# Query weights loaded plainly and turned by TensorE, late rows on GpSimd's queue, half of the key sums on GpSimd: a change to a two-layer linear-attention and GLU kernel

## The chip, the cores and the metric

The kernel runs on one core of a Trainium2 chip. Its engines work side by side, each on an instruction list of its own that it takes strictly in order, and meet through semaphores: TensorE (PE, matrix products), VectorE (DVE), ScalarE (ACT), GpSimd (POOL) and SyncE (SP, which here only issues DMAs). The metric is the time of one execution on the device, in microseconds (us); less is better.

## The reference

One sequence of 2048 rows (16 tiles of 128) by 512 features, in bf16. Two layers, each with an attention part and a GLU part; both layers use the same weights.

```python
def _A_ref(x, wqkv, w_phi, wo):                  # H = 32 heads, Dh = 16
    q, k, v = x @ wqkv, split by heads
    pq = einsum("bhsd,hdf->bhsf", q, w_phi); pk = the same with k
    phi_q = concat([softmax(pq), softmax(-pq)]); phi_k = concat([softmax(pk), softmax(-pk)])
    kv  = einsum("bhsf,bhsd->bhfd", phi_k, v);  z = phi_k summed over s
    num = einsum("bhqf,bhfd->bhqd", phi_q, kv); den = einsum("bhqf,bhf->bhq", phi_q, z) + 1e-6
    return (num / den) @ wo

def _B_ref(x, W_gate, W_up, W_down):             # F = 1376
    gate = x @ W_gate; up = x @ W_up
    return (relu(gate) * up) @ W_down

x = A_x
x = x + _A_ref(layernorm(x), ...);  x = x + _B_ref(layernorm(x), ...)
x = x + _A_ref(layernorm(x), ...);  x = x + _B_ref(layernorm(x), ...)
```

What sets the shape of the kernel: `kv` and `z` are sums over all 2048 rows, so no query can be answered before the keys and values of all 16 tiles are done.

## The kernel before

Everything stays in SBUF: x (16 tiles), all weights, and rings of buffers for what is in between. `build_kernel` records every operation with `op(...)`: its engine, a function that emits it, what it reads and writes, and two costs of the order's model, `ii` (how long it keeps its engine) and `lat` (when its result is there). `Program.forward` places the operations by a list of ranks, `RANKS`, one number per operation, and `prepare` turns the resulting order into waits on semaphores. `MOVED` lists operations that run on their second engine (`alt`). So the order on each engine is fixed by `RANKS`, `MOVED` and the model's costs; the chip then runs those lists in order, whatever the true times are.

At the start DVE builds an identity matrix, and PE runs 40 small matmuls that compute nothing (L553). `w_phi` is spread into block-diagonal form `BD` (L556, two parts on GpSimd and two on DVE). It is folded into the weights, so that one matmul gives the features before the softmax: `Wkp` = key weights times `BD`, `Wqp` = query weights times `BD` (`compose`, L586 for the matmuls, L462 and L463 for the copies from PSUM on ACT and DVE). This product needs the weights transposed. The key weights are loaded plainly into a part of `Wd` that is still free, and turned by PE (L574). The query weights are turned on the way by four DMA transposes from HBM (L521). SP issues the loads in the order of `LOADS`: x tile 0, key weights in two halves, x tile 1, tiles 2 and 3, value weights, tiles 4 to 7, query weights; then, between the transposes of later work, tiles 8 to 11 and 12 to 15 (`late_x`).

Then for each tile t of layer 0:
- `ln`: statistics and their aggregate on DVE (L600, L601), Ln and Exp on ACT (L603, L605), y on DVE (L620) or, for some tiles from 6 on, on GpSimd (L619; its small `nmr`, L616, is on GpSimd for tiles 6 to 15 in any case, and y waits for it even on DVE). y is turned by PE (L629) for tiles 0 to 3 and by a DMA transpose on SP (L634) for the others.
- `kv_tile`: keys K (L652, tile 0 at L656), two exponentials on ACT (L663), Z = sums of the exponentials in groups of 16 on DVE (L664), 1/Z on ACT by Ln and Exp (L668, L669), norm = their product on DVE (L672); values V (L681), copied to `vaug`, mostly by ACT (L462).
- `kv_sums`: the matmuls that sum over the tiles (L716), in bursts; then a mask on DVE (L724, L727) gives `kvs`.

Queries (`q_chunk`, L696, 16 chunks of four matmuls, exponentials at L700) depend only on y, so they can stand anywhere after it; PE uses some of them to fill the stage of keys and values. Then `attn_tile` for each tile (L749 products with `kvs`, small steps `sm` on GpSimd, DVE and ACT, t and o on DVE or GpSimd, L812 the output product, L815 the residual), and slab by slab the GLU (L842 gate and up, L849, L850, L870; L896 and L898 down; L904 the residual). Layer 1 has the same parts.

Of the kernel before, what the change touches and what calls it, by code (L numbers as in the profile page):

```python
# [12 lines left out]
P = 128  # L13
# [33 lines left out]
class Op:  # L47
    __slots__ = ("i", "eng", "fn", "ii", "lat", "tiles", "uses", "deps", "order", "succ", "start", "end",
                 "dma", "nbytes", "name", "alt", "cnt", "waits", "npend", "ready", "prio", "stream")


class Program:
    SYNC, START = 40.0, 750.0
    DMA_ISSUE, DMA_FIXED, DMA_BW = 470.0, 1500.0, 320.0
# [7 lines left out]
    def op(self, eng, fn, reads=(), writes=(), parts=(), ii=100.0, lat=None, name="", claims=(), after=(), dma=None, nbytes=0, alt=None):  # L62
# [6 lines left out]
        o.dma, o.nbytes, o.alt = dma, nbytes, alt  # L69
# [54 lines left out]
    def busy(self, o):  # L124
        return self.TR_ISSUE if o.dma == "tr" else self.DMA_ISSUE if o.dma else o.ii

    def lat(self, o):
        if o.dma == "tr":
            return self.TR_ISSUE + self.TR_FIXED + o.nbytes
        if o.dma:  # L130
            return self.DMA_ISSUE + self.DMA_FIXED + o.nbytes / self.DMA_BW
        return o.lat
# [21 lines left out]
    def forward(self, prio, look=60.0):  # L154
# [14 lines left out]
        bus = 0.0  # L169
# [31 lines left out]
        while left:  # L201
            pick = None
            for e in ENGINES:
# [5 lines left out]
                for o in ready[e]:  # L209
                    st = o.ready if o.ready > f else f  # L210
                    if low is not None and st > low + look:
                        continue
# [38 lines left out]
            elif o.dma:  # L251
                free[e] = st + self.DMA_ISSUE
                bus = max(bus, free[e]) + o.nbytes / self.DMA_BW
                o.end = bus + self.DMA_FIXED
            else:
                free[e] = st + o.ii
                o.end = st + o.lat
            for t in o.tiles:
# [86 lines left out]
    def prepare(self):  # L345
# [6 lines left out]
        ring = 0  # L352
        last_of = {}
        for o in self.sequence:
# [6 lines left out]
            if o.dma:  # L361
                o.stream = ("d", ring % self.n_dma_sems)
                ring += 1
# [45 lines left out]
def build_kernel(nc, A_x, A_wqkv, A_w_phi, A_wo, B_x, B_W_gate, B_W_up, B_W_down, out):  # L409
# [26 lines left out]
    eps = sb("eps", [1], FP32)  # L436
    kvs = sb("kvs", [8, 144])
# [57 lines left out]
    op("dve", lambda e: e.transpose(coli[:], rowi[:]), reads=rows, writes=[c_col], ii=100, lat=215, name="col")  # L495
    c_idq = [res("identq", q) for q in range(4)]
    for q in range(4):
        sl = slice(32 * q, 32 * q + 32)
        op("dve", lambda e, sl=sl: e.tensor_tensor(ident[sl, sl], rowi[sl, :], coli[sl, :], ALU.is_equal), reads=rows + [c_col, c_id], writes=[c_idq[q]], ii=90, lat=170, name="identq")
# [3 lines left out]
    op("dve", lambda e: e.memset(eps[:], 1e-5), writes=[c_eps], ii=35, lat=70, name="eps")  # L503

    xv = A_x.rearrange("b (t p) d -> p (b t) d", p=P)
    outv = out.rearrange("b (t p) d -> p (b t) d", p=P)
    chain = {"sp": [], "act": []}

    def load(eng, fn, writes, nbytes, name, after=()):
        o = op(eng, fn, parts=writes, dma="load", nbytes=nbytes, name=name, after=chain[eng][-1:] + list(after))  # L510
# [15 lines left out]
    wkn = Wd[:, 0:4, :]  # L526
# [4 lines left out]
    for q, what, *k in LOADS:  # L531
# [8 lines left out]
        elif what == "wvp":  # L540
            load(q, lambda e, k=k: e.dma_start(wv[:, k[0]:k[1], :], A_wqkv[k[0] * P:k[1] * P, 1024:1536].rearrange("(c p) f -> p c f", p=P)), [c_wv], 131072 * (k[1] - k[0]), "wv")
        elif what == "wq":
            for ic in range(4):
                load_wT(t_wq, c_wqT, 0, ic)
    late_x = []
    for t in range(8, 16, 4):
        load_x("sp", t, t + 4)
        late_x.append(chain["sp"][-1])

# [5 lines left out]
    for a in range(4):  # L555
        fn = lambda e, a=a: e.tensor_tensor(BD[:].rearrange("p c (a f b) -> p c a f b", f=16, b=2)[:, :, a], w128[:].unsqueeze(3).to_broadcast([P, 4, 16, 2]),  # L556
                                            m8[:, 2 * a:2 * a + 2].unsqueeze(1).unsqueeze(1).to_broadcast([P, 4, 16, 2]), ALU.mult)
        cost = {"pool": (290.0, 340.0), "dve": (190.0, 280.0)}
        here, other = ("pool", "dve") if a % 2 else ("dve", "pool")
        o_bd = op(here, fn, reads=[c_w128, c_m8], writes=[c_BD[a]], ii=cost[here][0], lat=cost[here][1], name="BD", alt=(other, fn) + cost[other])  # L560

    va_all = p_va.slots
    for i in range(16):
        op("pool", lambda e, i=i: e.memset(va_all[i][:, :, 128:130], 1.0), writes=[res("va1", i)], ii=60, name="vones", after=[o_bd])
    for i in range(2):
        op("pool", lambda e, i=i: e.memset(p_hr.slots[i], 0.0), writes=[res("hr0", i)], ii=500, name="hr0", after=[o_bd])
    op("pool", lambda e: e.tensor_copy(kvs[:, :, 136:144], mask2[:].unsqueeze(1).to_broadcast([P, 8, 8])), reads=[c_m2], writes=[res("kvsm")], ii=200, lat=280, after=[o_bd], name="kvsm")
# [510 lines left out]
```

## Time and profile before

The median of 6 runs is 394.4 us (392.17 to 395.38). The profiled execution took 394.61 us, of which its span, from first to last instruction, is 392.8; TensorE's granted clock was full throughout.

| Engine | busy us | share of the span | instructions |
|---|---|---|---|
| PE | 378.2 | 96% | 2413 |
| DVE | 298.3 | 76% | 641 |
| ACT | 195.3 | 50% | 606 |
| POOL | 42.1 | 11% | 117 |

Busy time by stretch of the span, in us:

| Stretch | PE | DVE | ACT | POOL |
|---|---|---|---|---|
| 0 to 10 | 7.88 | 8.16 | 5.68 | 2.84 |
| 10 to 20 | 8.00 | 8.06 | 8.17 | 0.00 |
| 20 to 30 | 9.41 | 9.65 | 9.66 | 1.72 |
| 30 to 40 | 10.00 | 9.88 | 9.34 | 5.39 |
| 40 to 55 | 14.33 | 14.25 | 12.31 | 0.00 |
| 55 to 90 | 32.29 | 31.39 | 21.77 | 6.65 |
| 90 to 210 | 119.37 | 92.14 | 50.82 | 7.76 |
| 210 to 260 | 47.92 | 42.13 | 34.07 | 4.77 |
| 260 to 392.8 | 128.96 | 82.61 | 43.49 | 13.02 |

A PE that shows busy is not a PE at its peak: a matmul's record includes the time in which its last results run out of the array, so the records of neighbours overlap and short gaps between them do not show. DVE's and ACT's records overlap in the same way, by some 0.1 us. Rows of the timeline give start, duration and a group of equal instructions; what stands in brackets is the idle time before the group and what ended it.

### The profile page before, as it was taken

The page shows a single profiled execution, that of the slowest core. Times are in us where ns is not written, and L with a number is a line of the kernel's source. Part 1 is how long each engine was busy: PE and PEld are TensorE (multiplying, and loading weights), DVE is VectorE, ACT ScalarE, POOL GpSimd, SP SyncE. Part 2 cuts the span into 40 slices and gives each one's busy share as a digit, 9 for nine tenths or more (in the row PEclk, how much of TensorE's full clock was granted, in tenths as well). Part 3 has the DMA queues.
Part 4 walks back from the last instruction along what each step waited for, and adds up shares of the span by engine and source line. Part 5 has one row for each costly group of instructions (what it writes and reads, how often), then busy time and mean ns, then how long its engine had stood idle before and what let it go on. Part 6 is the DMA issues. An engine that isn't in the chain of part 4 may idle for free.

```text
span 392.8 us, 6587 instructions
## 1 busy us (share of the span) xinstructions
PE 378.2 (96%) x2413; PEld 213.1 (54%) x2455; DVE 298.3 (76%) x641; ACT 195.3 (50%) x606; POOL 42.1 (11%) x117
## 2 busy tenths in 40 slices
PE   7799999899999999999999999999999999999996
PEld 6434565667655544444444457477865544544443
DVE  8899979899897769647678996889998648623424
ACT  5899969546544235334334574875634333113120
POOL 2016002111211000000000000233102110000000
PEclk9999999999999999999999999999999999999999
DMA  8464591233213321100202000013532221210102
GB/s 218 54 160 82 133 353 41 43 69 67 55 27 75 61 42 27 35 6 13 42 0 42 15 13 2 5 38 68 69 67 55 54 55 40 48 48 0 43 0 67
DMA packets 63008, 22.89 MB, mean 58 GB/s; under 512 B 53920, under 2 KB 62976, under 8 KB 62976
## 3 DMA queue, kind: packets, MB, share of 16 engines
q1 hardware_dynamic: 60144, 20.40, 24.2%
q10 hardware_dynamic: 2832, 2.08, 1.7%
q8 instruction: 19, 0.31, 0.3%
q14 instruction: 13, 0.11, 0.1%
HBM read 7.91 MB, written 2.10 MB: 25 GB/s over the span
## 4 chain that ended last, share of the span: by engine, by line
PE 78%; DVE 10%; DMA 4%; ACT 3%; SPq 2%; issue 1%; POOL 1%
PE pb L842 34%; PE pb L896 17%; PE pb L812 6%; PE pb L681 4%; PE pb L716 4%; PE pb L652 3%; PE pb L749 3%; PE pb L696 3%; PE pb L870 2%; DMA yT<-y 2%; PE pb L898 2%; DVE stats L600 2%; DVE t L786 2%; DMA yT<-in_A_wqkv_dram 2%; DVE z L664 1%; ACT expq L700 1%
## 5 line engine op out<-in xcount | busy, mean ns | idle before, releaser
L850 DVE TENSOR_TENSOR hT<-gate,pb 128x512 bf16<-128x512 bf16 (+1 forms) x100 | 57.2, 574 | 40.7 <-PE pb L842 36.0
L849 ACT ACTIVATE gate<-pb 128x512 bf16<-128x512 f32 (+1 forms) x100 | 50.9, 509 | 70.4 <-PE pb L842 69.9
L842 PE MATMUL pb<-yT,Wu 128*128 128x512 bf16 (+1 forms) x392 | 83.1, 336 | 0.3
L842 PE MATMUL pb<-yT,Wg 128*128 128x512 bf16 (+1 forms) x396 | 81.5, 336 | 0.3
L896 PE MATMUL pb<-Wd,hT 128*128 128x512 bf16 (+2 forms) x322 | 76.0, 372 | 0.3
L842 PEld LDWEIGHTS pb<-yT,Wg 128*128 128x128 bf16 x400 | 38.5, 98 | 29.2 <-DVE x_sb L815 0.3
L842 PEld LDWEIGHTS pb<-yT,Wu 128*128 128x128 bf16 x400 | 38.5, 98 | 28.7
L896 PEld LDWEIGHTS pb<-Wd,hT 128*128 128x128 bf16 x330 | 31.6, 98 | 35.1 <-ACT gate L849 0.3
L664 DVE TENSOR_REDUCE z<-phik 128x64 f32<-128x1024 bf16 x32 | 38.3, 1207 | 7.3 <-ACT phik L663 7.0
L600 DVE BATCH_NORM_STATS2 stats<-x_sb 128x6 f32<-128x512 bf16 x64 | 43.2, 684 | 0.5
L700 ACT ACTIVATE expq<-pb 128x512 bf16<-128x512 f32 x64 | 36.1, 610 | 13.8 <-PE pb L696 13.8
L663 ACT ACTIVATE phik<-pb 128x512 bf16<-128x512 f32 x64 | 35.6, 611 | 11.0 <-PE pb L652 10.9
L786 DVE TENSOR_TENSOR t<-pb,sm 128x384 bf16<-128x384 f32 x64 | 33.9, 548 | 0.8 <-POOL sm L776 0.5
L812 PE MATMUL pb<-wo,oT 128*128 128x512 bf16 x120 | 31.3, 379 | 2.3 <-ACT sm L775 1.3
L681 PE MATMUL pb<-wv,yT 128*128 128x512 bf16 x125 | 31.6, 379 | 1.6 <-DMA yT<-y 0.8
L603 ACT ACTIVATE lnv<-mv,eps 128x1 f32<-128x1 f32 (+1 forms) x58 | 16.9, 298 | 32.6 <-DVE mv L601 32.2
L904 DVE TENSOR_TENSOR x_sb<-x_sb,pb 128x512 bf16<-128x512 bf16 (+2 forms) x33 | 21.9, 663 | 12.7 <-PE pb L898 12.7
L696 PE MATMUL pb<-yT,Wqp 128*128 128x512 bf16 x124 | 31.0, 379 | 0.6 <-DVE t L786 0.3
L652 PE MATMUL pb<-Wkp,yT 128*128 128x512 bf16 x118 | 30.1, 379 | 0.9 <-DMA yT<-y 0.5
L620 DVE TENSOR_SCALAR y<-x_sb,mv,rstd 128x512 bf16<-128x512 bf16 x59 | 24.9, 424 | 4.6 <-ACT rstd L605 3.8
L763 ACT ACTIVATE sm<-pb 128x48 f32<-128x48 f32 (+1 forms) x96 | 15.6, 212 | 18.9 <-PE pb L749 18.9
L749 PE MATMUL pb<-kvs,expq 128*128 128x144 bf16 x256 | 23.9, 226 | 0.7 <-ACT expq L700 0.6
(77 smaller groups left out, 385.2 us busy)
## 6 DMA issues: line engine op xcount, KB each, us to landing
out_dram<-x_sb ACTq DMA_DIRECT2D x15, 128.0 KB, 1.7
x_sb<-in_A_x_dram SPq DMA_DIRECT2D x3, 512.0 KB, 4.1
Wg<-in_B_W_gate_dram SPq DMA_DIRECT2D x2, 640.0 KB, 7.2
Wu<-in_B_W_up_dram SPq DMA_DIRECT2D x2, 640.0 KB, 8.7
Wd<-in_B_W_down_dram SPq DMA_DIRECT2D x1, 1280.0 KB, 12.9
yT<-y SPq DMA_TRANSPOSE x55, 2.5
Wd<-in_A_wqkv_dram SPq DMA_DIRECT2D x2, 256.0 KB, 2.9
wv<-in_A_wqkv_dram SPq DMA_DIRECT2D x1, 512.0 KB, 6.6
```

Of the source, the lines that this page charges most:

```text
L600: op("dve", lambda e, t=t: e.bn_stats(stats[:, t, :], x_sb[:, t, :]), reads=[res("x", t)], writes=[res("st", t)], ii=600, lat=690, name=f" ...
L652: i = e.matmul(kt.ap(), src.ap()[:, ic, c0:c0 + 128], Wkp[:, ic, :], start=(ic == 0), stop=(ic == 3))
L664: op("dve", lambda e: e.tensor_reduce(zt.ap().rearrange("p (a b) -> p a b", b=2), ft.ap().rearrange("p s (a f b) -> p (s a) b f", f=16, b= ...
L681: i = e.matmul(vt.ap(), src.ap()[:, ic, c0:c0 + 128], wv[:, ic, :], start=(ic == 0), stop=(ic == 3))
L696: i = e.matmul(qt.ap(), Wqp[:, ic, c * 128:(c + 1) * 128], src.ap()[:, ic, :], start=(ic == 0), stop=(ic == 3))
L700: op("act", lambda e, g=g: e.activation(es[g][0].ap(), qt.ap(), ACT.Exp, scale=(1.0, -1.0)[g]), reads=[qr], writes=[es[g][1]], ii=477, lat ...
L786: return e.tensor_tensor(tt_.ap()[:, b, 0:384].rearrange("p (c h d) -> p c h d", h=8, d=16), pt.ap()[:, 0:432].rearrange("p (c w) -> p c w ...
L812: i = e.matmul(wt.ap(), oT_.ap()[:, c, :], wo[:, c, :], start=(c == 0), stop=(c == 3))
L842: i = e.matmul(pt.ap()[:, 0:n], W[:, ic, fc * 128:(fc + 1) * 128], src.ap()[:, ic, a * 128:b * 128], start=(ic == 0), stop=(ic == 3))
L849: op("act", lambda e: e.activation(st_.ap()[:, 0:n], gt.ap()[:, 0:n], ACT.Relu), reads=[gr], writes=[sr], ii=110 + n * .72, lat=230 + n * ...
L850: op("dve", lambda e: e.tensor_tensor(ht.ap()[:, a * 128:b * 128], st_.ap()[:, 0:n], ut.ap()[:, 0:n], ALU.mult), reads=[sr, ur], writes=[h ...
L896: i = e.matmul(pt.ap()[:, 0:n1 - n0], hT[l, s, fc].ap()[:, c:c + 128], Wd[:, fc, n0:n1], start=(fc == 0), stop=False)
```

## The change

- **Query weights**: loaded plainly by one DMA into another free part of `Wd` (`wqn`), sixth on SP where the value weights were, and turned by PE with 16 transposes (`turn`, the key weights' code made general). The four DMA transposes go. The value weights move to the end of `LOADS`.
- **Late rows**: x tiles 8 to 11 and 12 to 15 are loaded from GpSimd's queue, after tiles 4 to 7 have landed.
- **Z**: for tiles 3 to 13 of layer 0 (`POOL_Z`) GpSimd adds the two halves of each group of 16 exponentials into an fp32 tile of 512 columns (in a buffer of the ring `t`), and DVE reduces that over 8.
- **y**: `nmr` is on GpSimd from tile 4 on (`POOL_Y`), but only two y's of layer 0 run there, five before.
- **The order's model**: operations of DVE marked `port` are not placed while one of GpSimd's runs, and the other way round; some costs are new. GpSimd's memsets of `vaug` come after y of tile 0, those of `hr` and the copy of the mask after the keys of tile 8. GpSimd's DMAs have four semaphores of their own.
- **RANKS and MOVED** are new throughout, so the order of all engines is. What results, over the whole program, by the two orders: BD 4 on GpSimd (2 before) and 0 on DVE (2); copies of `Wkp` 4 on ACT (2) and 0 on DVE (2); copies of `vaug` 28 on ACT (23) and 4 on DVE (9), of which in layer 0 14 (16) on ACT; y on GpSimd 2 (5); o on GpSimd 16 (10) and on DVE 16 (22); `sm` steps on GpSimd 51 (67) and on DVE 45 (29). Query chunks that stand ahead of the last L716 of layer 0: 5 (6).

```diff
@@ Program @@
-    DMA_ISSUE, DMA_FIXED, DMA_BW = 470.0, 1500.0, 320.0
+    DMA_FIXED, DMA_BW = 1300.0, 285.0
...
                     st = o.ready if o.ready > f else f
+                    if e == "dve" and o.port and pool_end > st:
+                        st = pool_end
+                    elif e == "pool" and port_end > st:
+                        st = port_end
...
             if o.dma:
-                o.stream = ("d", ring % self.n_dma_sems)
-                ring += 1
+                if e == "pool":
+                    o.stream = ("d", self.n_dma_sems - 4 + soft % 4)
+                    soft += 1
+                else:
+                    o.stream = ("d", ring % (self.n_dma_sems - 4))
+                    ring += 1
@@ build_kernel @@
-    wkn = Wd[:, 0:4, :]
+    wkn, wqn, c_wqn = Wd[:, 0:4, :], Wd[:, 4:8, :], res("wqn")
...
+        elif what == "wqn":
+            load(q, lambda e: e.dma_start(wqn, A_wqkv[:, 0:512].rearrange("(c p) f -> p c f", p=P)), [c_wqn], 524288, "wqn", after=k[0] if k else ())
...
-    late_x = []
-    for t in range(8, 16, 4):
-        load_x("sp", t, t + 4)
-        late_x.append(chain["sp"][-1])
+    for t in (8, 12):
+        k = res("x", 7) if ("sp", "wqn") in LOADS else c_wqT[2 if t == 8 else 3]
+        load("pool", lambda e, t=t: e.dma_start(x_sb[:, t:t + 4, :], xv[:, t:t + 4, :]), [res("x", k) for k in range(t, t + 4)], 524288, f"x{t}", after=k.writers)
...
+    def turn(src, rd, dst, wr, name, engs):
+        for ic in range(4):
+            pt, pres = tile(p_ps, name, ic)
+            def mmt(e, ic=ic, pt=pt):
+                for c in range(4):
+                    i = e.transpose(pt.ap().bitcast(BF16)[:, c * 128:(c + 1) * 128], src(ic)[:, c * 128:(c + 1) * 128], ident[:])
+                return i
+            op("pe", mmt, reads=rd(ic) + c_id, writes=[pres], ii=240, lat=400, name=f"{name} mm")
+            op_copy(engs[ic], lambda ic=ic: dst.ap()[:, :, ic * 128:(ic + 1) * 128], lambda pt=pt: pt.ap().bitcast(BF16)[:, 0:512].rearrange("p (c n) -> p c n", c=4), [pres], [wr[ic]], f"{name} cp", True)
+    turn(lambda ic: wkn[:, ic, :], lambda ic: [c_wkn[ic], c_wd], t_wk, c_wkT, "WkT", ["act", "dve", "act", "dve"])
+    if ("sp", "wqn") in LOADS or ("pool", "wqn") in LOADS:
+        turn(lambda ic: wqn[:, ic, :], lambda ic: [c_wqn, c_wd], t_wq, c_wqT, "WqT", ["act", "dve", "act", "dve"])
...
-        op("dve", lambda e: e.tensor_reduce(zt.ap().rearrange("p (a b) -> p a b", b=2), ft.ap().rearrange("p s (a f b) -> p (s a) b f", f=16, b=2), AX.X, ALU.add),
-           reads=fr2, writes=[zr], ii=1105, lat=1185, name=f"Z{l}.{t}")
+        if (l, t) in POOL_Z:
+            ht_, hr_ = tile(p_t, "zh", l, t)
+            zh = lambda: ht_.ap().rearrange("p a b -> p (a b)").bitcast(FP32)
+            v = lambda: ft.ap().rearrange("p s (a f b) -> p (s a) f b", f=16, b=2)
+            op("pool", lambda e: e.tensor_tensor(zh().rearrange("p (a b f) -> p a f b", f=8, b=2), v()[:, :, 0:8, :], v()[:, :, 8:16, :], ALU.add), reads=fr2, writes=[hr_], ii=1110, lat=1154, name=f"Zp{l}.{t}")
+            op("dve", lambda e: e.tensor_reduce(zt.ap(), zh().rearrange("p (q f) -> p q f", f=8), AX.X, ALU.add), reads=[hr_], writes=[zr], ii=590, lat=670, name=f"Zh{l}.{t}")
+            zr = [zr]
+        else:
...
+    for i in range(16):
+        op("pool", lambda e, i=i: e.memset(va_all[i][:, :, 128:130], 1.0), writes=[res("va1", i)], ii=60, name="vones", after=[yop[0, 0]])
     for t in range(NT):
         kv_tile(0, t)
-    for k, o in enumerate(late_x):
-        pr.behind(o, next(d for d in pr.ops if d.name == f"yT0.{4 + 2 * k}"))
+    for i in range(2):
+        op("pool", lambda e, i=i: e.memset(p_hr.slots[i], 0.0), writes=[res("hr0", i)], ii=500, name="hr0", after=[kop[0, 8]])
...
+POOL_Z = {(0, t) for t in range(3, 14)}
-POOL_Y = {(0, t) for t in range(6, 16)}
+POOL_Y = {(0, t) for t in range(4, 16)}
...
-    ("sp", "x", 0, 1), ("act", "wphi"), ("sp", "wk", 0, 2), ("sp", "wk", 2, 4), ("sp", "x", 1, 2), ("sp", "x", 2, 4), ("sp", "wv"), ("sp", "x", 4, 8), ("sp", "wq"),
+    ("sp", "x", 0, 1), ("act", "wphi"), ("sp", "wk", 0, 2), ("sp", "wk", 2, 4), ("sp", "x", 1, 2), ("sp", "x", 2, 4), ("sp", "wqn"), ("sp", "x", 4, 8), ("sp", "wv"),
```

The `port` mark stands on BD, y, norm, o and the `sm` steps `p`, `den` and `coef`. A switch in `ln` that would put Ln and Exp on GpSimd (`POW_LN`) is empty and emits nothing but one small memset.

## The prediction

> **What bounds it now.** I read the busy row first: PE is busy 96% of the span, but a matmul's record carries its pipeline tail, so I priced PE by the distance between starts in the chain of waits:
>
> ```profile
> 51.47 3.72 PE pb L716 x64
> ...
> 105.17 4.32 PE pb L842 x20
> ```
>
> A 512-column matmul takes 4.32/20 = 0.216 us, a 129-column one 3.72/64 = 0.058. By the same division 256 columns take 0.109, 192 take 0.0825, 144 take 0.063, 128 take 0.056. Times the program's counts (1,344 of 512 columns, 320 of 256, 128 of 192, 256 of 129, 256 of 144, 100 small ones after 40 for warming) this is 372.5 us of PE work. PE's first matmul starts at 1.08 and its last ends at 389.65, so PE stands still for 16 us in all. Taking each group's start in the PE timeline from the end of the work before it places them: 6.2 us before 20, 2.0 from 20 to 40, none from 40 to 60, 3.9 from 60 to 90, 3.1 from 210 to 260, under 1 in the rest. These gaps are all that any change here can win, besides 3 us at the end. The first of them, in PE's timeline (start, duration, group, and the wait before it):
>
> ```profile
> 9.84 1.04 PE L681 MATMUL pb<-wv,yT 128*128 128x512 bf16 x4 [0.73 <-DMA wv<-in_A_wqkv_dram]
> 10.72 0.39 PE L629 MATMUL pb<-ident,y 128*128 128x128 bf16 x4
> 11.98 0.40 PE L586 MATMUL pb<-BD,yT 128*128 128x128 bf16 x4 [0.87 <-DMA yT<-in_A_wqkv_dram]
> 12.21 1.03 PE L652 MATMUL pb<-Wkp,yT 128*128 128x512 bf16 x4
> 14.31 0.40 PE L586 MATMUL pb<-BD,yT 128*128 128x128 bf16 x4 [1.07 <-DMA yT<-in_A_wqkv_dram]
> ```
>
> PE takes its instructions in order. L586 composes the query weights out of the transposed rows that four DMA transposes bring, and what is queued behind it (the keys of tiles 1 to 3) waits too. PE is busy without a gap only from 18. The queue that issues those DMAs:
>
> ```profile
> 3.67 0.51 SPq L515 DMA_DIRECT2D x_sb<-in_A_x_dram  x1
> 4.22 7.27 SPq L521 DMA_TRANSPOSE yT<-in_A_wqkv_dram  x4
> 18.39 1.19 SPq L634 DMA_TRANSPOSE yT<-y  x1
> 19.63 0.58 SPq L515 DMA_DIRECT2D x_sb<-in_A_x_dram  x1
> ...
> 25.80 0.58 SPq L515 DMA_DIRECT2D x_sb<-in_A_x_dram  x1
> ```
>
> From 20 to 54 PE, ACT and DVE are all full: in the windows DVE is busy 9.65 us of 20 to 30, 9.88 of 30 to 40 and 14.25 of 40 to 55. DVE's last norm (L672) ends at 53.69 and PE's last L716 at 55.2, so DVE ends the stage of keys and values, while PE fills its time with query chunks (six before 55.2). A stage that ends earlier thus gains only if PE also loses its gaps.
>
> **The change, part by part.** What moves is read from the two orders, instruction by instruction. Line numbers are those of before.
>
> 1. **Query weights.** Four DMA transposes (7.27 us of SP's queue) go. In wv's old place, sixth on SP, stands a plain load of the same 512 KB, so I take its landing at 9.8, where the row above shows wv's. PE gains 16 transposes: 16 x 0.056 = 0.9 us of work. PE's order is now: key matmuls of tile 0, 12 weight transposes (waiting for that load until 9.8, as L681 did), y1, 4 more, 4 of L586, y2, 4 of L586, y3, keys 1 to 3, values 0 and 1, 4 of L586, values 2 and 3, 4 of L586. The two waits of 0.87 and 1.07 us go. What is late next is ACT, which copies weights and y (0.48 us from one start to the next): five copies from 10.2 end at 12.7; keys 1 to 3 run 11.8 to 14.4, values 0 to 3 and the rest of L586 to 18.3. Before, the same work (keys and values 0 to 3, all L586) was done at 20.07. **Lead: 1.8 us**, the 0.9 us included.
> Of transposes the Trainium skill says (VectorE: DVE Perf Modes, The three transpose paths) that 128x128 takes 390 ns on TensorE and 1309 ns on the DMA crossbar. By it, 16 on PE would cost 6.2 us and turn the lead into a loss; the trace's rows of four take 0.39 us in all when PE has them queued, so I use the row. The crossbar figure is near the 1.2 us of issue here, but one instruction here turns four such blocks.
>
> 2. **Value weights** are now last on SP, behind rows 4 to 7. The window 5 to 10 moved 259 GB/s, which is 2 us for each 512 KB: rows 4 to 7 land at about 11.5 (their stats ran at 11.40 before, from the same place in the queue) and wv at 13.5. PE wants it at 14.4, behind keys 1 to 3: hidden, with 0.9 us to spare.
>
> 3. **Late rows on GpSimd's queue**, both after rows 4 to 7 have landed. Before, they were issued at 19.63 and 25.80 behind SP's transposes, and no wait of DVE stands behind them, so the load itself gains nothing. The trace has no DMA from GpSimd. From below, like SP's (median 4.1 us from issue to landing): 15.5 and 17.5. DVE now wants row 8 at 16.2 and row 12 at 19.5: hidden. The skill speaks against it (SBUF — State Buffer, SBUF: two separate sides): a DMA from GpSimd has its descriptors written by GpSimd's cores and starves while VectorE runs an operation in a 2-port mode. By it each y (0.40 us) in the way holds a load up; at most three of them run between 11.5 and 15, so 1.2 us is the upper end and the load lands by 16.7. Row 8 would then cost DVE 0.5 us at most; I take 0. Behind the two issues stand GpSimd's nmr for tiles 4 to 7, for which y4 on DVE now waits: two issues at SP's 0.58 us end at 12.7, at twice that at 13.8, and y4's other inputs are there at 14.3. Hidden; if an issue took three times SP's, y4 would be 0.7 us late and so would its transpose. SP's own queue is empty from 4.2, so y4's transpose starts when y4 is done (14.8) and lands at 17.3 (2.5 us, the page); PE wants it at 18.3.
>
> 4. **Z on GpSimd.** For tiles 3 to 13 half of L664 becomes a GpSimd add of 512 results, then a half-length DVE reduce. The nearest rows:
>
> ```profile
> L664 DVE TENSOR_REDUCE z<-phik 128x64 f32<-128x1024 bf16 x32 | 38.3, 1207 | 7.3 <-ACT phik L663 7.0
> ...
> L796 POOL TENSOR_TENSOR o<-t 128x512 bf16<-128x512 bf16 x10 | 11.6, 1164 | 25.6 <-DVE t L791 13.7 <-DVE t L786 11.9
> ```
>
> GpSimd: 11 x 1.16 = 12.8 us, with nmr, y and memsets 18.8. DVE in the chain's distances: Z 1.13, half 0.6, norm 0.6, stats 0.615, y 0.33, aggr 0.11. After y4 and y5 (15.1) DVE has 5 Z 5.65, 11 halves 6.6, 16 norms 9.7, 8 stats 4.9, 8 aggr 0.9, 8 y 2.6, three casts 1.8: 32.2 us, so 47.3 without stalls, against 53.69.
> But norm, y and GpSimd shut each other out:
>
> ```profile
> 33.85 1.52 POOL L619 TENSOR_SCALAR y<-x_sb,rstd,nmr 128x512 bf16<-128x512 bf16 x2
> ...
> 34.80 1.70 DVE L672 TENSOR_TENSOR phik<-phik,rz 128x1024 bf16<-128x1024 bf16 x2
> ...
> 39.81 2.48 DVE L672 TENSOR_TENSOR phik<-phik,rz 128x1024 bf16<-128x1024 bf16 x4
> ```
>
> Two norms take 1.28 us alone (four take 2.48); here 1.70, as the first is held until GpSimd ends at 35.37. The skill has it as a lock for the whole instruction (SBUF — State Buffer, Who interferes with whom): by the rule, 24 norms and y's that arrive at random meet GpSimd busy 18.8 of 32.2 us, with half an add (0.58) left: 0.34 each, 8.1 us. By the rows it is less: from 21 to 38 GpSimd worked 5.9 us and DVE lost 0.42 there, 0.45 at 30.11 (a y of 0.85) and 0.34 waiting for nmr, a fifth. A fifth of 18.8 is **3.8 us, my value**, as the new order sets reduces and stats beside the adds; ends 0 and 8.1. The last norm then ends at 51.1 and the last L716 about 1.5 later, 52.6. PE's own sum from 18.3 is 24 key and value groups 20.75, five query chunks 4.3, L716 7.4: 50.8. ACT's (31 exponentials, 14 vaug, 3 Wqp, 10 expq at 0.48, plus small ones 6.7) ends at 47 plus waits. I take 52.8 for the last L716, against 55.2; one query chunk fewer (0.86) is done by then. **Gain 1.6 us**, the lead of part 1 inside it.
>
> 5. **After that.** Now L749 of tiles 0 and 1 follows the last L716 directly; before, one chunk stood between and hid the masking of kvs (54.42 to 56.03). PE waits some 0.8 us there. But two more chunks (11, not 9) are left to fill the 3.9 us of gaps from 60 to 90. I take 1.3 us of those filled: **net gain 0.5**, ends -1 and +1.5. The rest is reordered, with six more o's on GpSimd (1.16 against 0.43) and 16 small sm steps back on DVE: 0, with 1.5 either way, since only 3.5 us of gaps lie there.
>
> 6. **BD** all on GpSimd: 3.32 + 4 x 0.45 = 5.1, DVE 0.6 us less; L586 wants them at 6.4: 0. All four Wkp copies on ACT (2.0 us from 6.7) let the first keys run to 8.9, against 9.1: 0. The moved memsets, 60 semaphores instead of 64 for SP and ACT, and the constants of the order's model run nothing on the path: 0.
>
> **Sum:** 1.6 + 0.5 = 2.1 us from the profiled execution of 394.6 (span 392.8 and 1.8 around it): 392.5. That run lies 0.2 above the median of 394.4, so **392.3**.
>
> **Rivals.**
> - **The port ends the stage** (slower). Place: DVE's norms from 30 to 52. At 8.1 us of stalls the last norm ends at 55.4, L716 at 56.9: 2.5 us past the 54.4 that breaks even (55.2 less the chunk); with part 5 at 0 it gives 396.9. It decides from 5.6 us of stalls, 0.23 per norm and y. For it: GpSimd's share; against: one fifth measured, and ACT paces the tiles at 1.9 us, so stalls can hide. 0.17.
> - **The start was hidden anyway.** The lead is lost again because ACT and DVE set the pace to 54 as before: 394.3. For it: three full engines. 0.14.
> - **No stall to speak of**: the last L716 at 51.3, 1.5 us more, and later gaps shrink by 0.5 more: 390.3. For it: 6.4 us of DVE work gone. 0.19.
> - Mine, 392.3, itself 390.8 to 393.8: 0.50.
>
> **From these:** a measurement of this kernel tells about 0.5% (2 us) from no change, so faster is below 392.4: all 0.19 of the last rival, 0.31 of mine, 0.02 of the hidden start, 0.52. Slower is above 396.4: 0.11 of the port case, and 0.06 of mine and 0.03 of the hidden start where the reordering behind 60 us loses more than part 5 allows: 0.20. Between: 0.28. The range runs from 389.2 to 396.5, from the last rival less the 1.1 left of part 5's bound to just under the port case.
>
> **What will show it.** PE has values 0 to 3 and the whole composition done near 18.3, and no composing matmul waits for a DMA; the first value matmul waits for none either; the last matmul of the kv sums ends near 52.8; norms run longer than 0.69 us where the Z add is on GpSimd, by 3.8 us in sum with the y's; PE stands some 0.8 us between the kv sums and the third group of L749. I am wrong if norms and y's wait over 5.6 us, if the query load lands past 11, or if gaps appear beyond 90 us, where I priced nothing.

## The result and the profile after

| | before | changed |
|---|---|---|
| median, us | 394.42 (391.4 to 395.76, 42 runs) | 391.77 (390.56 to 393.58, 21 runs) |
| ratio, 95% interval | | 0.9939 [0.9925, 0.9953] |
| profiled execution, us (span) | 394.61 (392.8) | 391.08 (389.3) |
| value and key stage: PE's last matmul of the kv sums ends | 55.2 | 51.44 |

The change makes the kernel 0.6% faster, 2.6 us by the medians and 3.5 by the two profiled executions. The forecast was 392.3. Lines of code moved with the change: L585 and L599 turn and compose weights (before L574, L586), L671 and L709 are keys and values (L652, L681), L687 and L688 the two halves of the new Z, L700 the norm (L672), L744 the kv sums (L716), L777 the products (L749), L840 the output product (L812), L898 the rest of gate and up (L870). In some experiments an added line moves them by a few more.

PE's timeline of the changed kernel, at its start and at the end of the stage of keys and values (start, duration, group; in brackets the idle time before it and what ended that):

```profile
9.83 0.84 PE L585 MATMUL pb<-ident,Wd 128*128 128x128 bf16 x12 [0.92 <-DMA Wd<-in_A_wqkv_dram]
...
11.40 0.39 PE L599 MATMUL pb<-BD,yT 128*128 128x128 bf16 x4
...
11.85 2.76 PE L671 MATMUL pb<-Wkp,yT 128*128 128x512 bf16 x11
14.45 1.89 PE L709 MATMUL pb<-wv,yT 128*128 128x512 bf16 x8
...
18.13 0.39 PE L599 MATMUL pb<-BD,yT 128*128 128x128 bf16 x4
...
47.56 3.88 PE L744 MATMUL pb<-vaug,phik 128*128 128x129 bf16 x64
51.27 1.19 PE L777 MATMUL pb<-kvs,expq 128*128 128x144 bf16 x16
52.51 1.67 PE L724 MATMUL pb<-yT,Wqp 128*128 128x512 bf16 x7
```

One wait is left at the start, for the plain load of the query weights. The composition, and with it the keys and values of tiles 0 to 3, is done at 18.4 (18.13 and four times 0.056); before, the same work was done at 20.07. The values at 14.45 wait for no load. From 18.5 to the end of the kv sums PE has no wait over 0.05 us: its own work now ends the stage. DVE's last norm ends at 49.31, 2.1 us ahead of it.

The groups of the changed kernel from 15 to 52 us (busy time, mean ns of one, and the idle time before them with what ended it), DVE's three and then GpSimd's one:

```profile
L700 DVE TENSOR_TENSOR phik<-phik,rz 128x1024 bf16<-128x1024 bf16 x16 | 11.8, 776 | 0.2 <-ACT rz L697 0.2
L688 DVE TENSOR_REDUCE z<-t 128x64 f32<-128x512 f32 x11 | 7.4, 670 | 0.0
...
L639 DVE TENSOR_SCALAR y<-x_sb,mv,rstd 128x512 bf16<-128x512 bf16 x9 | 4.2, 486 | 0.0
```

```profile
L687 POOL TENSOR_TENSOR t<-phik 128x512 f32<-128x512 bf16 x11 | 14.5, 1334 | 4.9 <-DVE z L688 3.8 <-ACT phik L682 1.1
```

DVE still hardly waits in this stage, but has less to do. Norms and y's are longer than alone (681 and 403 ns in an experiment below), and so are GpSimd's adds (1,334 ns; an add that nothing held takes 1,150): DVE and GpSimd hold each other up. Further on stands what I had not priced. The chain of waits around 257 and 309 us (two stretches of one view; start, duration, what):

```profile
257.57 4.11 DMA oT<-o
...
262.03 0.82 PE pb L840 x3
```

```profile
309.35 3.85 DMA yT<-y
313.20 0.05 issue
313.25 0.83 PE pb L898 x8
```

Two DMA transposes take 4.11 and 3.85 us from issue to landing, where the median is 2.5, and PE stands 1.27 and 0.72 us for them. Neither wait is in the profile of before.

### The profile page after: what moved, and what is told of

It reads as the page before. It is cut to its first block, busy times and chain, and to the rows that moved or that the text cites. A ratio compares the mean times of both kernels' runs of the same rounds, so it can differ in the third digit from the quotient of the medians.

```text
span 389.3 us, 6649 instructions
## 1 busy us (share of the span) xinstructions
PE 377.5 (97%) x2427; PEld 214.1 (55%) x2471; DVE 289.8 (74%) x645; ACT 198.6 (51%) x617; POOL 59.1 (15%) x122
## 4 chain that ended last, share of the span: by engine, by line
PE 84%; ACT 5%; DVE 5%; DMA 4%; issue 1%; SPq 1%; POOL 0%
PE pb L870 33%; PE pb L924 17%; PE pb L709 7%; PE pb L671 7%; PE pb L840 6%; PE pb L724 4%; PE pb L744 4%; PE pb L777 3%; ACT expq L728 3%; PE pb L898 2%; PE pb L926 2%; DMA Wd<-in_A_wqkv_dram 2%; DMA oT<-o 1%; DMA yT<-y 1%; DVE x_sb L843 1%
## 5 line engine op out<-in xcount | busy, mean ns | idle before, releaser
L870 PE MATMUL pb<-yT,Wu 128*128 128x512 bf16 (+1 forms) x395 | 82.1, 336 | 0.2
L870 PE MATMUL pb<-yT,Wg 128*128 128x512 bf16 (+1 forms) x397 | 81.0, 336 | 0.3
L924 PE MATMUL pb<-Wd,hT 128*128 128x512 bf16 (+2 forms) x319 | 75.2, 372 | 0.5
L870 PEld LDWEIGHTS pb<-yT,Wg 128*128 128x128 bf16 x400 | 38.6, 98 | 30.3 <-ACT gate L877 0.4
L870 PEld LDWEIGHTS pb<-yT,Wu 128*128 128x128 bf16 x400 | 38.7, 98 | 29.9 <-DVE t L814 0.2
L840 PE MATMUL pb<-wo,oT 128*128 128x512 bf16 x118 | 30.7, 379 | 2.6 <-DMA oT<-o 1.3
L709 PE MATMUL pb<-wv,yT 128*128 128x512 bf16 x126 | 30.8, 379 | 0.1
L724 PE MATMUL pb<-yT,Wqp 128*128 128x512 bf16 x121 | 29.9, 379 | 0.6 <-DVE t L819 0.2
L671 PE MATMUL pb<-Wkp,yT 128*128 128x512 bf16 x119 | 29.6, 379 | 0.3
L804 POOL TENSOR_TENSOR sm<-sm 128x64 f32<-128x64 f32 x18 | 5.8, 324 | 148.1 <-ACT sm L803 148.1
L791 ACT ACTIVATE sm<-pb 128x48 f32<-128x48 f32 (+1 forms) x96 | 16.4, 221 | 21.6 <-PE pb L777 21.3
L691 DVE TENSOR_REDUCE z<-phik 128x64 f32<-128x1024 bf16 x21 | 24.8, 1203 | 0.6 <-ACT phik L682 0.6
```

What stands on the lines that cost most here:

```text
L671: i = e.matmul(kt.ap(), src.ap()[:, ic, c0:c0 + 128], Wkp[:, ic, :], start=(ic == 0), stop=(ic == 3))
L709: i = e.matmul(vt.ap(), src.ap()[:, ic, c0:c0 + 128], wv[:, ic, :], start=(ic == 0), stop=(ic == 3))
L724: i = e.matmul(qt.ap(), Wqp[:, ic, c * 128:(c + 1) * 128], src.ap()[:, ic, :], start=(ic == 0), stop=(ic == 3))
L840: i = e.matmul(wt.ap(), oT_.ap()[:, c, :], wo[:, c, :], start=(c == 0), stop=(c == 3))
L870: i = e.matmul(pt.ap()[:, 0:n], W[:, ic, fc * 128:(fc + 1) * 128], src.ap()[:, ic, a * 128:b * 128], start=(ic == 0), stop=(ic == 3))
L924: i = e.matmul(pt.ap()[:, 0:n1 - n0], hT[l, s, fc].ap()[:, c:c + 128], Wd[:, fc, n0:n1], start=(fc == 0), stop=False)
```

## The experiments

All ran beside the kernel before, whose median was 394.1 to 394.3 in each set. Except where a line says otherwise, an edit keeps the changed kernel's order on every engine.

**Query weights by DMA transposes again.** The sixth load is wv again, the four DMA transposes come back behind it, the 16 transposes on PE and their four copies go.

```diff
-    ..., ("sp", "wqn"), ("sp", "x", 4, 8), ("sp", "wv"),
+    ..., ("sp", "wv"), ("sp", "x", 4, 8), ("sp", "wq"),
```

> The changed kernel with the query weights as before: value weights sixth on SP, then rows 4 to 7, then four DMA transposes of the query weights; PE's 16 transposes and their 4 copies are left out, every other operation keeps its place on its engine. Theory (the query part gives the lead at the start and PE sets the end of the kv stage): the composing matmuls wait for DMA transposes near 12 and 14.3 us, keys 1 to 3 start near 14.5 instead of 11.85, PE has values 0 to 3 done near 20 instead of 18.35, the kv sums end near 53.1 instead of 51.4, time 393.5. Rival (the start is hidden, DVE or ACT set the end of the stage): kv sums still near 51.5, time 391.8.

Measured: 391.26 us (389.25 to 394.01), ratio 0.9923 [0.9887, 0.996]. PE's timeline of this kernel:

```profile
11.74 0.40 PE L599 MATMUL pb<-BD,yT 128*128 128x128 bf16 x4 [1.59 <-DMA yT<-in_A_wqkv_dram]
...
48.78 3.87 PE L744 MATMUL pb<-vaug,phik 128*128 128x129 bf16 x64
```

One wait of 1.59 us at the start is back, not two, and the kv sums end at 52.65, 1.2 later than in the changed kernel, nearly as expected. Yet the whole is no slower: in its profile the two waits after 257 us are missing. The interval is too wide for a figure, but the expected loss did not come. Something after the stage gives the 1.2 us back, and this kernel has 32 instructions fewer on PE.

**Z wholly on DVE.**

```diff
-POOL_Z = {(0, t) for t in range(3, 14)}
+POOL_Z = set()
```

> The changed kernel with Z of tiles 3 to 13 reduced in full on DVE, in the place of the half-length reduce; GpSimd's 11 adds are left out, all else keeps its place. Theory (without GpSimd's help DVE ends the kv stage): DVE has 11 x 0.53 = 5.8 us more of reduces and loses its 2.3 us of port stalls, so its last norm ends near 52.8 instead of 49.3 and the kv sums near 54.7 instead of 51.4; time 394.5 to 395. Rival (PE alone sets the stage and DVE has slack): kv sums within 0.5 us of 51.4, time 391.8 to 392.3.

Measured: 395.81 us, ratio 1.0036 [1.0018, 1.0055]; PE's timeline:

```profile
50.64 5.44 PE L744 MATMUL pb<-vaug,phik 128*128 128x129 bf16 x64 [2.24 <-DVE phik L700]
```

Now PE waits for DVE's norms ahead of the last kv sums, which end at 56.08, 4.6 later; 3.3 had been expected. Moving half of Z is worth about 4 us (395.81 against 391.77), and without it the change gains nothing. Here GpSimd adds nothing, so this trace also has norms and y's alone: means of 681 and 403 ns.

**Late rows in their old places**: from SP's queue, behind the first and the fourth y transpose.

```diff
-        load("pool", lambda e, t=t: e.dma_start(x_sb[:, t:t + 4, :], ...), ..., after=k.writers)
+        load("sp", lambda e, t=t: e.dma_start(x_sb[:, t:t + 4, :], ...), ...)
```

> The changed kernel with rows 8 to 11 and 12 to 15 loaded from SP again, behind the first and the fourth DMA transpose of y as before; all else keeps its place. By the prediction's sentence that the load itself gains nothing: time 391.8, no change. By the rival that the new order lives on early rows: the load of rows 8 to 11 is issued near 16.1 and lands near 20, DVE waits for it some 4 us at 16.2, and unless the stage has slack the kv sums end 2 to 4 us later, time 394 to 395.5.

Measured: 400.78 us, ratio 1.0164 [1.0131, 1.0197]. DVE's timeline:

```profile
19.59 0.69 DVE L613 BATCH_NORM_STATS2 stats<-x_sb 128x6 f32<-128x512 bf16 x1 [3.93 <-DMA x_sb<-in_A_x_dram]
...
27.45 1.28 DVE L613 BATCH_NORM_STATS2 stats<-x_sb 128x6 f32<-128x512 bf16 x2 [5.05 <-DMA x_sb<-in_A_x_dram]
```

The two loads are issued at 15.6 and 23.2 and take 4 us. DVE stands 9 us, and the kv sums end at 60.8. The expectation had counted the first of the two waits alone. The new order wants row 8 at 16.2: it can't do without early rows.

**The same rows early, but from SP's queue**, right behind wv, waiting for rows 4 to 7 as in the changed kernel.

```diff
-        load("pool", lambda e, t=t: ..., after=k.writers)
+        load("sp", lambda e, t=t: ..., after=k.writers)
```

> The changed kernel, with rows 8 to 15 loaded as early as there, but from SP's queue, right behind the value weights, instead of GpSimd's. It tells the queue from the time: e3 changed both. My theory (only the time counts): rows 8 and 12 land by 16.2 and 19.5 from either queue, nothing on SP stands behind these two issues until y4's transpose is wanted at 14.9, and the nmr of tiles 4 to 7 on GpSimd is free of two issues of 0.84 us: 391.8, within 0.8. Rival (GpSimd's queue itself is needed): the two waiting issues hold SP so that y4's transpose is issued past 15.5, or the rows come past 16.5: the kv sums end past 52.5 and it takes 393 or more.

Measured: 391.28 us, ratio 0.9929 [0.9906, 0.9951]. SP's queue and, below, DVE:

```profile
4.76 4.05 SPq L565 DMA_DIRECT2D x_sb<-in_A_x_dram  x2
15.11 1.29 SPq L653 DMA_TRANSPOSE yT<-y  x1
```

```profile
16.45 0.68 DVE L613 BATCH_NORM_STATS2 stats<-x_sb 128x6 f32<-128x512 bf16 x1
```

Row 8 is there when DVE wants it, y4's transpose goes out at 15.1. The time of the load counts (9 us), the queue does not.

**Z on GpSimd in the kernel before**, in that kernel's order, for the same tiles.

```diff
@@ before.py, kv_tile @@
-        op("dve", lambda e: e.tensor_reduce(...), reads=fr2, writes=[zr], ..., name=f"Z{l}.{t}")
+        op("pool", lambda e: e.tensor_tensor(...), reads=fr2, writes=[hr_], ..., name=f"Zp{l}.{t}")
+        op("dve", lambda e: e.tensor_reduce(...), reads=[hr_], writes=[zr], ..., name=f"Zh{l}.{t}")
```

> The kernel before with the Z part alone: Z of tiles 3 to 13 split between GpSimd and DVE, every other operation keeps its place of before. Theory (Z on GpSimd is of use only with a PE order that has no waits of its own): the waits at the start stay, of PE's 2.0 us of gaps from 20 to 40 only some go, time 393.3 to 394.4. Rival (Z on GpSimd is the whole gain): 391.8. Rival (port): DVE's norms and y's wait for GpSimd more than 5 us, time above 395.

Measured: 397.34 us, ratio 1.0076 [1.0048, 1.0103]; the kv sums end at 58.0. Its groups from 20 to 58 us on DVE:

```profile
L679 DVE TENSOR_TENSOR phik<-phik,rz 128x1024 bf16<-128x1024 bf16 x15 | 10.3, 717 | 0.0
L669 DVE TENSOR_REDUCE z<-t 128x64 f32<-128x512 f32 x11 | 7.5, 678 | 7.1 <-POOL t L668 7.1
...
L620 DVE TENSOR_SCALAR y<-x_sb,mv,rstd 128x512 bf16<-128x512 bf16 x5 | 2.4, 495 | 1.5 <-POOL nmr L616 1.5
```

The time is that of the port rival, but the norms are hardly held (717 ns), so the port is not to blame. The old order asks for the short reduce where it asked for the whole one, before GpSimd has the sum: DVE stands 7.1 us for it, and 1.5 for nmr behind it on GpSimd. In this order moving Z costs 3 us; in the new one it is worth 4.

**The fetch of PE's instructions.** The missing waits of the first experiment led to a second theory. In the page of the changed kernel, the DMA queues have these two (packets, MB, share of 16 engines):

```profile
q8 instruction: 19, 0.31, 0.3%
q14 instruction: 13, 0.11, 0.1%
```

The Trainium skill (Runtime: NRT & Kernel Launch, Instruction fetch mechanics) says that an engine's instructions come by DMA in blocks of 16 KB, 256 instructions each, and that this is mostly hidden. The trace fits that for q8 and PE: 19 packets of 16,384 bytes for PE's 4,898 instructions (19 times 256 is 4,864), and from one packet to the next PE starts some 250. No wait of PE in the profile is put down to them. But the DMA engines have other work then. In the records of the single packets, block and transpose lie so (us):

```
kernel            block, took      the transpose's 544 packets                      PE waits
changed           259.65, 0.94     542 in 258.74-259.65, the last two after that    1.27 at 262.03
before            217.34, 0.93     542 in 216.48-217.39, the last two at 218.26     0.76 at 219.42
fewer (below)      34.57, 1.25     542 in  33.74-34.64,  the last two at  35.80     1.54 at  36.99
more (below)      273.70, 1.36     the last 42 at 275.05-275.89, begun 273.51       1.34 at 276.65
```

A transpose has 544 packets, 512 of 256 bytes and 32 of 4. In the first three rows only two packets of 4 bytes come behind the block, in the last row 42 packets, and each time the whole transpose lands late. Which of the 16 DMA engines moved a packet the records do not tell. The rest of the changed kernel's trace fits: of its 87 transposes issued after 20 us, 13 were under way when a block came, and six of these took 3.85 to 4.62 us to land; of the other 74 none took over 3.28.

If this is right, a block comes when PE has had a certain number of instructions. So it can be moved, with the same work, by the warming matmuls at the start: 16 of 256 columns for 32 of 128 (fewer; the zeros that they read are made 256 wide), or 32 of 64 for 16 of 128 (more).

```diff
@@ fewer @@
-    for k in range(WARM):
-        op("pe", lambda e: e.matmul(pt_w.ap()[:, 0:128], wm.ap()[:, 0:128], wm.ap()[:, 0:128], ...), ...)
+    for k in range(24):
+        n = 256 if k < 16 else 128
+        op("pe", lambda e, n=n: e.matmul(pt_w.ap()[:, 0:n], wm.ap()[:, 0:128], wm.ap()[:, 0:n], ...), ...)
@@ more @@
+    for k in range(56):
+        n = 64 if k < 32 else 128
...
```

The changed kernel once more, for comparison:

> The changed kernel itself, run beside the next three for a direct comparison on one chip. All theories: 391.8, within 0.7. In its profiled run PE stood 1.2 us at 260.8 (for an oT transpose that took 4.1 us from issue to landing instead of 2.5) and 0.8 at 312.4 (for a yT transpose). Theory F (fetch): both come from the 16 KB blocks of PE's own instructions that the DMA engines fetch (at 259.65, 0.94 us; at 310.75, 1.02 us), which hold up the last packets of a transpose under way; then this profile shows the fetches at the same places in the program and at least one of the two waits again. Theory C (chance): the waits are scatter, and lie elsewhere or nowhere in this profile.

With fewer and with more instructions:

> The changed kernel, with the first 32 warming matmuls of 128 columns made 16 of 256: the same time at the start, but 32 fewer instructions on PE (16 weight loads and 16 matmuls), so every later block of PE's instructions is fetched some 16 matmuls later in the program (about 1.5 us near 260). Theory F: the fetch near 260 then falls at about 261.2 and the one near 311 at about 312.3, past the transposes that PE waits for; the waits of 1.2 and 0.8 us go and it takes 389.8 to 390.5. Theory C: nothing changes, 391.8.

> The changed kernel, with 16 of the warming matmuls made 32 of 64 columns: the same time at the start, 32 more instructions on PE, so that every fetch comes some 16 matmuls earlier (about 1.5 us near 260: at 258.1, beside the first half of the oT transpose; near 311: at 309.2, between two transposes). Theory F: the wait near 260 shrinks below 0.7 us or goes, the one near 312 goes: 390 to 391.2, if no new collision appears elsewhere. Theory C: 391.8.

| | median, us | lowest to highest | ratio, 95% |
|---|---|---|---|
| changed again | 391.37 | 390.84 to 392.76 | 0.9936 [0.9913, 0.996] |
| 32 fewer | 390.38 | 389.84 to 390.62 | 0.9907 [0.9886, 0.9928] |
| 32 more | 392.99 | 392.02 to 393.6 | 0.9976 [0.996, 0.9992] |

PE's timelines of the three, in this order:

```profile
262.18 1.02 PE L840 MATMUL pb<-wo,oT 128*128 128x512 bf16 x4 [1.17 <-DMA oT<-o]
```

```profile
36.99 1.04 PE L672 MATMUL pb<-Wkp,yT 128*128 128x512 bf16 x4 [1.54 <-DMA yT<-y]
...
261.68 1.03 PE L841 MATMUL pb<-wo,oT 128*128 128x512 bf16 x4
```

```profile
263.42 1.03 PE L841 MATMUL pb<-wo,oT 128*128 128x512 bf16 x4
...
276.65 1.02 PE L841 MATMUL pb<-wo,oT 128*128 128x512 bf16 x4 [1.34 <-DMA oT<-o]
```

Repeated, the changed kernel has the block at 259.88 and the wait at the same matmul; the wait near 313 is down to some 0.3 us. With fewer instructions the block comes at 262.22 and both waits are gone; a new one, at 36.99, is hidden only in part (the kv sums end at 52.5, 0.8 later), and the kernel is 1.0 us faster than the changed one beside it, with no run in common. With more, the block comes at 260.76 and the wait for this product is gone as expected, but blocks meet other transposes: three new waits, 0.69 at 78.81, 0.92 at 111.15 and the one shown, each beside a block. My 390 to 391.2 held only if no new collision came, and three came. Some 0.5 us of its loss comes earlier, though: its kv sums end at 52.2, not 51.7, behind a wait of 0.76 for a norm, and no block is shown to be the cause of that. By L898's start, which is at 259.25, 260.08 and 261.82 in the three kernels, the block moved by +1.5 and by -1.7 us of PE's work, where 1.5 had been expected.

Two readings over all the profiles leave little to chance. Every one with the changed kernel's number of PE instructions (its own two and six of experiments) has this wait, of 0.98 to 1.27 us; the three with another number do not. And from the end of the kv sums to its end the changed kernel takes 337.8 us (337.6 again), the one with fewer 335.7, and the first experiment, also 32 instructions short, 335.7 too.

**The first experiment with the blocks put back**: DMA transposes for the query weights, and the 32 lost instructions made up by warming matmuls of half the width.

> e1 (the changed kernel with the query weights turned by DMA transposes again), with the 32 PE instructions that it lost beside the changed kernel put back as warming matmuls of half the width (16 of 128 columns made 32 of 64). PE's fetches then fall at the same places of the program as in the changed kernel. Theory F: e1 was as fast as the changed kernel only because its fetches missed the transposes; now the start costs its 1.2 us and the later waits return in part or whole: 392.6 to 393.3. Rival: the query part is worth nothing, whatever the fetches: as e1, 391.3.

Measured: 396.18 us (393.14 to 397.59), ratio 1.0058 [1.0033, 1.0082]. Its timeline on PE, and windows of 2 us (busy PE, PEld, DVE, ACT, POOL, then the granted clock, the DMA share and GB/s):

```profile
13.59 0.61 PE L600 MATMUL pb<-BD,yT 128*128 128x128 bf16 x4 [3.72 <-DMA yT<-in_A_wqkv_dram]
...
266.84 1.02 PE L841 MATMUL pb<-wo,oT 128*128 128x512 bf16 x4 [0.98 <-DMA oT<-o]
...
318.34 0.83 PE L899 MATMUL pb<-Wr,yT 128*128 128x192 bf16 x8 [0.79 <-DMA yT<-y]
```

```profile
12.00:14.00 2.00, 0.41 (x5) 0.42 (x6) 1.87 (x7) 0.00 (x0) 0.94 (x2) 0.50 0.86 199
14.00:16.00 2.00, 2.00 (x16) 1.57 (x15) 0.00 (x0) 1.09 (x2) 0.00 (x0) 0.50 1.03 328
```

The two late waits return, as expected, and from the end of the kv sums to its end this kernel takes 337.9 us again. More than expected happens at the start: the block at 10.82 (1.17 us) meets the query weights' own transposes, PE stands 3.72 us instead of 1.59, its granted clock falls to half until about 18, and the kv sums end at 56.5. So the query part is worth 1.2 us at the kv sums where no block meets the transposes and 4.8 (56.5 against 51.7 in the changed kernel again) where one does.

**The kernel before with fewer instructions**, by the same edit.

> The kernel before, with the first 32 warming matmuls of 128 columns made 16 of 256 (32 fewer instructions on PE, the same time at the start), as e6 did to the changed kernel. In the profile of before, the fetch at 12.16 lies on the fourth DMA transpose of the query weights, whose last 43 packets come at 13.24 to 14.09 (PE waits 1.07 us for it), and the fetch at 217.34 on a y transpose whose last two packets come at 218.26 (PE waits 0.76). Theory F: with the fetches some 16 matmuls later both waits go; the second is worth its 0.8 us, the first at most its 1.1, since DVE ends that stage: 392.8 to 393.8, if no new collision appears. Theory C: 394.2.

Measured: 392.91 us (391.92 to 396.04), ratio 0.9982 [0.9961, 1.0004]. PE's timeline:

```profile
11.32 0.40 PE L587 MATMUL pb<-BD,yT 128*128 128x128 bf16 x4 [0.80 <-DMA yT<-in_A_wqkv_dram]
...
12.42 0.39 PE L587 MATMUL pb<-BD,yT 128*128 128x128 bf16 x4
...
72.03 1.02 PE L813 MATMUL pb<-wo,oT 128*128 128x512 bf16 x4 [1.10 <-DMA oT<-o]
```

The kernel before had two such waits of 0.87 and 1.07 us at the start, as the prediction's rows show, and further on this one:

```profile
219.42 1.04 PE L681 MATMUL pb<-wv,yT 128*128 128x512 bf16 x4 [0.76 <-DMA yT<-y]
```

The second at the start and this one are gone, with both blocks elsewhere; a block at 69.71 brings a wait of 1.10 at 72.03. The kv sums end at 53.4, 1.8 earlier, where at most 1.1 had been expected; the composing matmuls also start 0.66 us sooner. The median falls into the expected range; the interval still touches 1, so a gain of the whole is not shown.

**Who holds whom.** Behind each of the eleven Z adds GpSimd does extra work on idle buffers that nothing reads: an add that reads SBUF, or two memsets, which only write. (Two memsets ahead of all this fill the buffers that the add reads.)

```diff
@@ kv_tile, behind Zp: reading @@
+            op("pool", lambda e: e.tensor_tensor(scr[2][0].ap(), scr[0][0].ap(), scr[1][0].ap(), ALU.add), ...)
@@ kv_tile, behind Zp: writing @@
+            [op("pool", lambda e, i=i: e.memset(scr[i][0].ap(), 0.0), ...) for i in range(2)]
```

> The changed kernel, with one more GpSimd add of two bf16 tiles of 512 columns behind each of the eleven Z adds (idle buffers, the result is used nowhere): some 1.16 us each, 12.8 us more GpSimd work that reads SBUF between 16 and 47. Theory P (while GpSimd reads SBUF, DVE's norms and y's are held, and it while they run): the stalls go from 2.3 us to 5 or more, norms average over 0.85 us against 0.776, the kv sums end past 53.5 instead of 51.44: 393.5 to 396. Theory Q (a busy GpSimd alone holds the rest up, since nmr and the next Z add stand behind the extra work): the same loss here and in the next kernel.

> As the one before, but the extra work behind each Z add is two memsets of 512 columns (some 0.52 us each, 11.4 us in all), which write SBUF and read nothing. Theory P: norms stay near 0.78 us, the kv sums end within 1 us of 51.44, below the kernel with the reading add by 1.5 us or more: 391.8 to 392.8. Theory Q: as the one before, within 0.8 us.

Measured: 399.49 us with adds, ratio 1.0133 [1.0108, 1.0157], and 395.06 with memsets, 1.0014 [0.9993, 1.0034]. The kv sums end at 60.6 and 54.4. With adds, a norm on DVE and GpSimd beside it:

```profile
34.49 1.63 DVE L704 TENSOR_TENSOR phik<-phik,rz 128x1024 bf16<-128x1024 bf16 x1
```

```profile
34.38 1.20 POOL L690 TENSOR_TENSOR t<-phik 128x512 f32<-128x512 bf16 x1
35.53 1.60 POOL L691 TENSOR_TENSOR hT<-hT 128x512 bf16<-128x512 bf16 x1
```

The norm begins at 34.49 in the middle of an add, and ends at 36.12, 0.54 us after the add's end at 35.58; the next add, begun at 35.53, takes 1.60 instead of 1.15, since it is held while the norm runs. They take turns, whole instructions long. With memsets:

```profile
32.77 1.62 DVE L702 TENSOR_TENSOR phik<-phik,rz 128x1024 bf16<-128x1024 bf16 x1
...
44.44 0.68 DVE L702 TENSOR_TENSOR phik<-phik,rz 128x1024 bf16<-128x1024 bf16 x1
```

```profile
32.67 1.18 POOL L688 TENSOR_TENSOR t<-phik 128x512 f32<-128x512 bf16 x1
33.79 0.98 POOL L689 MEMSET hT<- 128x512 bf16 x2
...
43.98 0.98 POOL L689 MEMSET hT<- 128x512 bf16 x2
```

A norm beside memsets takes 0.68, as alone; one that meets a Z add is held until 33.85 and then runs beside the memset. That is what the Trainium skill says (SBUF — State Buffer, Who interferes with whom): a DVE instruction with two SBUF inputs contends with a GpSimd instruction that reads SBUF, not with one that only writes it. Neither theory had the sizes right. The memsets cost some 3.3 us against the changed kernel's 391.8 all the same, and the adds 4.4 us more. Without holds eleven adds are 11 x 1.15 = 12.7 us of GpSimd's time, 22 memsets 22 x 0.52 = 11.5: the 1.2 us between them are too little for 4.4, so that is mainly the reads. In the memset kernel the norms from 13 to 50 us average 1,011 ns, though no memset holds one: the Z adds lie otherwise, and five of these 13 norms, which meet one, take 1.36 to 1.64 us (in the changed kernel three norms in all were held, to 0.92, 1.04 and 1.63). That the adds of the changed kernel fall more luckily because they wait 3.8 us for DVE's short reduce is likely from this, but not shown.

## Why the prediction was right, and where not

The time was right (392.3 for 391.8), inside the range and on the right side. Its parts were not all so, and that the number came so near is in part luck.

1. **Query weights: right in the trace, half told in its worth.** The load landed at 9.83 for 9.8, composition and values were done at 18.4 for 18.3. What the lead is worth I had inside the stage's 1.6 us. It is 1.2 at the kv sums. But I took before's waits of 0.87 and 1.07 for the DMA transposes' own slowness; the second is a fetched block (gone in the kernel before with fewer instructions). The part's other worth, 3.6 us more where a block hits those transposes, was in no term.
2. **Value weights: right**, no wait.
3. **Late rows: the landing right, the worth wrong.** They took 4.1 and 5.4 us to land, and row 8's statistics ran at 16.20 without a wait. But "the load itself gains nothing" was read from the order of before, which never waited for them; in the new order it is worth 9 us. Both numbers stood in my own step (row 8 wanted at 16.2, issued at 19.63 before) and I did not subtract them.
4. **Z: right in the mechanism, mis-sized in the stall, and so wrong in what ends the stage.** I put 3.8 us; norms cost (776 - 681) x 16 = 1.5 and y's (486 - 403) x 9 = 0.7, 2.3 in all. The last norm ended at 49.31 for 51.1, the kv sums at 51.44 for 52.8. With 3.8 us of stalls DVE's norms would have ended the stage; with 2.3 PE's own work did, for which my sum had said 50.8. The time is that of the rival without stalls (51.3), but not its reason: there were stalls, and PE hid them. The share of a fifth was read from a stretch with y's on GpSimd, and misread: from 21 to 38 the trace has 7.1 us of GpSimd work, not 5.9, which makes a sixth, or 3.2 us. The rest lies in how the adds fell: 2.3 of 20.3 us of GpSimd work from 15 to 50, a ninth. The loss is also two-sided, which I had not counted: GpSimd's eleven adds lost 0.18 us each, off the path here.
5. **After that: the sum near, the places wrong.** The stage gained 3.8 us, 2.9 with the one chunk fewer; the spans differ by 3.5, so what came later gained 0.6 for my 0.5. But PE stood only 0.2 us at the products, not 0.8 (the 16 of L777 from 51.27 fill 1.0, the next group starts at 52.51). And beyond 90 us, where I said gaps would prove me wrong, there are two of 1.27 and 0.72. These 2.0 us are waits for transposes that a fetched block met. Without them, and without the one such wait of before that went (0.76 at 219.42), the part behind the stage would have gained some 1.8 us (0.6 + 2.0 - 0.76).
6. **BD, copies, memsets: right at 0**, as far as the trace shows: nothing waits for them.

So the forecast was helped by two misses of opposite sign: the stall term 1.5 us too large, and 2 us of waits for transposes with no term at all. Where these two waits are gone (fewer instructions), the changed kernel takes 390.4, outside the 390.8 to 393.8 of my own case. That version beats both kernels, the one before by 0.9% [0.7, 1.1] and the changed one by 1.0 us.

## What to carry to other kernels

In this kernel, with 4,898 instructions on PE, an edit that changed their number by 32 moved the later instruction blocks, and with them which DMA transposes landed 1 to 2 us late. Where a kernel has as long a list and as many transposes, the same is to be looked for: before crediting or blaming an edit for one or two microseconds, look whether a wait elsewhere came or went, and run it with the count of instructions put back. A new order makes new needs: price each load by when the new order wants it, not by whether the old one waited. Work moved to GpSimd cost both engines time here (norms 776 ns for 681, adds 1,334 for 1,150), and paid only with an order that asks for its result later.

## What the runs showed of the hardware that was not expected

- The same work with 32 instructions more or fewer on PE, at the start, makes 393.0 or 390.4 us where the changed kernel takes 391.4, for the most part through blocks of 16 KB (0.9 to 1.6 us each) that hold back a few of a DMA transpose's packets; six in the changed kernel landed 3.9 to 4.6 us after issue, where the median is 2.5. Two late packets of 4 bytes are enough. Why a transpose whose last two packets are moved at 35.80 to 35.83 lands only at 36.94 stays open.
- After PE had stood for 3.72 us, the granted clock was 0.50 from 12 to 16 us, and four composing matmuls took 0.61 us for 0.40; a late load thus costs PE more than its wait. In the kernel with late rows in their old places a wait of 4.63 us had the same effect (0.50 from 28 to 34), and in the one with the extra adds a wait of 4.49 (0.66 as a mean from 50 to 60).
- GpSimd issues a load of 512 KB in 0.84 us and it lands 4.7 us after; SP issues one in 0.58 and it lands after 4.1. This difference cost nothing here.
